# A transformer layer on one core: SyncE's waits for loads and transposes move from ahead of the last eight stores to behind the last transpose

## The chip, the core and the metric

The kernel runs on one core of a Trainium2 chip. The metric is the device time of the whole program in microseconds (us); less is better. Engines are called TensorE (PE), VectorE (DVE), ScalarE (ACT), GpSimd (POOL) and SyncE (SP). SyncE does no arithmetic here: it issues DMA transfers and waits on semaphores, in the order of its queue.

## The reference

One layer of a transformer over 2048 tokens of 448 features, in bfloat16: linear attention with 16 heads of 28, whose feature map is a pair of softmaxes, and a gated feed-forward part of width 1792. Both read a layer norm, and both are added to their input.

```
q, k, v = split(layernorm(x) @ wqkv)                      # 16 heads of 28
phi(a)  = concat(softmax(a @ w_phi), softmax(-(a @ w_phi)))
kv, z   = phi(k)^T @ v, sum(phi(k))
o       = (phi(q) @ kv) / (phi(q) . z + 1e-6)
h       = x + o @ wo
n       = layernorm(h)
out     = h + (sigmoid(n @ w_gate) * (n @ w_up)) @ w_down
```

## The kernel before

The 2048 tokens are 16 tiles of 128 rows. Attention goes tile by tile; the feed-forward part goes by chunks of 2, 4, 4, 4 and 2 tiles (0-1, 2-5, 6-9, 10-13, 14-15). For each chunk TensorE makes the gate and up products (the helper at L514), ScalarE takes tanh (L845), VectorE the product (L852); then, for each tile, TensorE multiplies by `w_down` (L871) into a PSUM bank, VectorE adds that to the residual in `x_sb` (L878, task `fin`), and a DMA writes the tile to the output (L880, task `st`). The two tiles of the last chunk are finished and stored in two parts each: 336 columns (`fina`, `sta`, called wide here) and 112 columns (`finb`, `stb`, narrow).

The kernel is written as a graph of named tasks. `PLAN` is a list of task numbers, written out by hand: the one order in which all tasks are emitted, from which each engine gets its own queue. `emit` walks that list. For each task it first puts into the engine's queue the waits for what the task needs, then the task itself. A wait that the same engine has already made for the same or a higher value is left out (`seen`).

Three kinds of DMA task have rings of semaphores: `in` (24 loads, a semaphore each), `tr` (39 transposes by DMA, 12 semaphores) and `out` (18 stores, 8 semaphores). A task whose ring has gone round waits first for the transfer that used its semaphore before. The walk counts in `nring` how many of each kind it has met. At one point it makes SyncE wait for the last transfer on every `in` and `tr` semaphore: 24 + 12 waits. At the end of the program SyncE waits for the last store on each `out` semaphore.

All loads and transposes and 17 of the 18 stores are in SyncE's queue. By `PLAN` its last part is this, in order (`hT` is the transpose of a normed tile, L810):

```
hT 14, st 5, hT 15, st 8, st 6, sta 15, st 7,
        st 9, st 10, st 12, st 11, st 13, sta 14, stb 14
```

`hT 15` is the last of the 39 transposes. `st 9` is the eleventh store of 18. `stb 15` is in ScalarE's queue, between `sta 14` and `stb 14` in `PLAN`. VectorE's last tasks are, in order, `fin 10`, `fin 12`, `fina 15`, `fin 11`, `fin 13`, `fina 14`, `finb 15`, `finb 14`.

Of the kernel before, what the change touches and what calls it, by code (L numbers as in the profile page):

```python
# [79 lines left out]
class _Graph:  # L80
# [67 lines left out]
    def emit(self, rings):  # L148

        nc = self.nc  # L150
        done = self.planned()
        queues = {e: [] for e in self.ENGINES}
        with ExitStack() as es:
            sems = {e: es.enter_context(nc.semaphore("s_" + e)) for e in self.ENGINES if e != "sp"}
            ring_sems = {k: [es.enter_context(nc.semaphore("s_%s%d" % (k, i))) for i in range(n)]
                         for k, n in rings.items()}
            count = {e: 0 for e in self.ENGINES}
            nring = {k: 0 for k in rings}
            ticket = {}
            seen = {}  # L160

            def wait(eng, sem, key, val):
                if seen.get((eng, key), 0) >= val:
                    return
                seen[(eng, key)] = val
                queues[eng].append(lambda e, sem=sem, val=val: e.wait_ge(sem, val))

            n_out = sum(t.kind == "out" for t in done)
            for t in done:
                if t.kind == "out" and nring.get("out", 0) == n_out - 8:  # L170

                    assert nring["in"] == rings["in"]
                    for k in ("in", "tr"):
                        for j in range(min(nring[k], rings[k])):
                            wait("sp", ring_sems[k][j], (k, j), 16 * ((nring[k] - 1 - j) // rings[k] + 1))
                top = {}
                for d in t.need:
                    sem, key, val, eng = ticket[d]
                    if eng == t.eng == "pe" and d not in t.ordered:
                        continue  # L180
                    if key not in top or top[key][1] < val:
                        top[key] = (sem, val)
                for key, (sem, val) in top.items():
                    wait(t.eng, sem, key, val)
                if t.kind is not None:
                    j = nring[t.kind]
                    nring[t.kind] += 1
                    n = rings[t.kind]
                    sem, key = ring_sems[t.kind][j % n], (t.kind, j % n)
                    if j >= n:  # L190
                        wait(t.eng, sem, key, 16 * (j // n))
                    queues[t.eng].append(lambda e, t=t, sem=sem: t.fn(e).then_inc(sem, 16))
                    ticket[t.name] = (sem, key, 16 * (j // n + 1), "dma")
                else:
                    count[t.eng] += 1
                    sem = sems[t.eng]
                    queues[t.eng].append(lambda e, t=t, sem=sem: t.fn(e).then_inc(sem, 1))
                    ticket[t.name] = (sem, t.eng, count[t.eng], t.eng)

            last = {}  # L200
            for t in done:
                if t.kind == "out":
                    sem, key, val, _ = ticket[t.name]
                    last.pop(key, None)
                    last[key] = (sem, val)
            for key, (sem, val) in last.items():
                wait("sp", sem, key, val)
            with nc.Block() as block:
                starters = {"sp": block.sync, "act": block.scalar, "pe": block.tensor, "dve": block.vector,
                            "pool": block.gpsimd}  # L210
                for e in self.ENGINES:
                    def run(eng, q=queues[e]):
                        for f in q:
                            f(eng)
                    starters[e](run)
# [705 lines left out]
```

## Time and profile before

| | |
|---|---|
| median of 3 runs | 206.84 us (206.36 to 206.85) |
| the profiled execution | 206.24 us |
| its span, first to last instruction | 204.5 us |
| TensorE busy | 196.8 us, 96% of the span |
| VectorE, ScalarE, GpSimd busy | 132.7, 96.0, 79.0 us |
| granted TensorE clock | 1.00 |
| stores on SyncE, issue to landing, median | 1.8 us |

The lines of the profile name an engine, a line of the kernel, an operation and what it writes and reads (`out<-in`). `SPq` is an instruction in SyncE's queue. For a DMA the time shown is that of the issue; its landing is told separately. Times in a timeline count from the first instruction. `EVENT_SEMAPHORE` is an instruction that only waits on semaphores (L166 is the line of the kernel's `wait`); a wait can also be carried by the instruction that it holds. Single records may be missing from a trace.

### The profile page before, as it was taken

The page shows a single profiled execution, that of the slowest core. Times are in us where ns is not written, and L with a number is a line of the kernel's source. Part 1 is how long each engine was busy: PE and PEld are TensorE (multiplying, and loading weights), DVE is VectorE, ACT ScalarE, POOL GpSimd, SP SyncE. Part 2 cuts the span into 40 slices and gives each one's busy share as a digit, 9 for nine tenths or more (in the row PEclk, how much of TensorE's full clock was granted, in tenths as well). Part 3 has the DMA queues.
Part 4 walks back from the last instruction along what each step waited for, and adds up shares of the span by engine and source line. Part 5 has one row for each costly group of instructions (what it writes and reads, how often), then busy time and mean ns, then how long its engine had stood idle before and what let it go on. Part 6 is the DMA issues. An engine that isn't in the chain of part 4 may idle for free.

```text
span 204.5 us, 5003 instructions
## 1 busy us (share of the span) xinstructions
PE 196.8 (96%) x2029; PEld 106.5 (52%) x2029; DVE 132.7 (65%) x306; ACT 96.0 (47%) x182; POOL 79.0 (39%) x141
## 2 busy tenths in 40 slices
PE   7899999999999998999999999999999999999993
PEld 3444454445377764555555544444544444886562
DVE  2999999898799979729574466465128345543033
ACT  3789999998983580423342042423002443551000
POOL 8569999768759865600830003003000300000000
PEclk9999999999999999999999999999999999999999
DMA  5999997059683955191155151013200004000014
GB/s 147 272 268 222 307 383 215 0 110 340 135 132 75 188 88 104 44 168 40 40 114 103 30 103 27 24 27 27 72 0 0 3 11 109 3 3 0 0 42 140
DMA packets 49751, 21.06 MB, mean 103 GB/s; under 512 B 40512, under 2 KB 48704, under 8 KB 49728
## 3 DMA queue, kind: packets, MB, share of 16 engines
q1 hardware_dynamic: 49584, 20.71, 44.6%
q8 instruction: 16, 0.26, 0.5%
q14 instruction: 7, 0.06, 0.1%
q10 hardware_dynamic: 144, 0.03, 0.1%
HBM read 9.20 MB, written 1.84 MB: 54 GB/s over the span
## 4 chain that ended last, share of the span: by engine, by line
PE 76%; ACT 7%; DVE 6%; POOL 5%; issue 2%; DMA 2%; SPq 1%; DVEq 0%; POOLq 0%; ACTq 0%
PE ps L514 51%; PE ps L871 21%; POOL hh L619 3%; ACT eq L654 2%; ACT hh L599 2%; DVE ssum L612 2%; DMA wphK<-in_A_w_phi_dram 2%; PE ps L705 1%; DVE hh L619 1%; POOL rs L543 1%; DVE x_sb L878 1%; PE ps L585 1%; SPq L358 1%; DVE sq L671 1%; PE ps L475 1%
## 5 line engine op out<-in xcount | busy, mean ns | idle before, releaser
L514 PE MATMUL ps<-xT,wg_sb 64*128 64x512 bf16 (+1 forms) x490 | 87.0, 333 | 1.1 <-DVE x_sb L878 0.7
L514 PE MATMUL ps<-xT,wu_sb 64*128 64x512 bf16 (+1 forms) x490 | 86.8, 333 | 0.0
L845 ACT ACTIVATE tg<-ps 128x512 f32<-128x512 f32 (+1 forms) x70 | 33.9, 511 | 76.8 <-PE ps L514 76.1
L852 DVE SCALAR_TENSOR_TENSOR hh<-tg,ps 128x512 bf16<-128x512 f32 (+1 forms) x70 | 38.2, 573 | 32.1 <-ACT tg L845 31.9
L514 PEld LDWEIGHTS ps<-xT,wg_sb 64*128 64x128 bf16 x490 | 45.6, 94 | 22.7 <-issue 1.9
L514 PEld LDWEIGHTS ps<-xT,wu_sb 64*128 64x128 bf16 x490 | 45.6, 94 | 15.2
L871 PE MATMUL ps<-wd_sb,hh 128*128 128x448 bf16 (+2 forms) x252 | 43.5, 332 | 0.0
L871 PEld LDWEIGHTS ps<-wd_sb,hh 128*128 128x128 bf16 x252 | 22.9, 98 | 19.3 <-issue 1.0
L878 DVE SCALAR_TENSOR_TENSOR x_sb<-ps,x_sb 128x448 bf16<-128x448 f32 (+2 forms) x18 | 10.0, 566 | 24.4 <-PE ps L871 24.4
L775 POOL TENSOR_SCALAR rs<-mv 128x1 f32<-128x1 f32 x14 | 2.7, 192 | 59.7 <-DVE mv L774 58.8
L619 POOL TENSOR_TENSOR hh<-hh,rsum 128x896 bf16<-128x896 bf16 x13 | 21.9, 1700 | 0.5 <-DVE rsum L615 0.5
L599 ACT ACTIVATE hh<-ps,rs 128x448 bf16<-128x448 f32 x32 | 18.7, 643 | 2.0 <-PE ps L585 1.1
L654 ACT ACTIVATE eq<-ps,rs 128x448 bf16<-128x448 f32 x32 | 18.1, 649 | 0.0
L612 DVE TENSOR_REDUCE ssum<-hh 128x32 f32<-128x896 bf16 x16 | 16.9, 1058 | 0.8 <-ACT hh L599 0.6
L668 POOL TENSOR_TENSOR halves<-eq 128x448 f32<-128x448 bf16 x14 | 13.4, 970 | 8.3 <-DVE sq L671 2.7
L514 PE MATMUL ps<-Wvc,xT 64*128 64x448 bf16 x112 | 13.2, 351 | 0.2
L681 POOL TENSOR_TENSOR eq<-eq,rq 128x448 bf16<-128x448 bf16 x14 | 13.0, 942 | 1.0 <-DVE eq L681 0.8
L514 PE MATMUL ps<-Wq,xT 64*128 64x448 bf16 x112 | 13.1, 351 | 0.1
L514 PE MATMUL ps<-Wk,xT 64*128 64x448 bf16 x98 | 11.5, 351 | 0.2
L514 PE MATMUL ps<-wo_sb,oT 64*128 64x448 bf16 x98 | 11.3, 350 | 0.1
L790 ACT ACTIVATE hn<-x_sb,nb,rs 128x512 bf16<-128x512 bf16 x10 | 7.8, 810 | 5.5 <-POOL nb L788 3.0
L715 DVE TENSOR_TENSOR o_pad<-ps,rden 128x448 bf16<-128x448 f32 x16 | 9.8, 620 | 0.2
(104 smaller groups left out, 186.4 us busy)
## 6 DMA issues: line engine op xcount, KB each, us to landing
wu_sb<-in_B_w_up_dram SPq DMA_DIRECT2D x2, 896.0 KB, 8.2
wg_sb<-in_B_w_gate_dram SPq DMA_DIRECT2D x2, 896.0 KB, 7.5
out_dram<-x_sb SPq DMA_DIRECT2D x14, 112.0 KB, 1.8
x_sb<-in_A_x_dram SPq DMA_DIRECT2D x3, 448.0 KB, 4.1
wd_sb<-in_B_w_down_dram SPq DMA_DIRECT2D x3, 448.0 KB, 4.6
hh<-in_A_wqkv_dram SPq DMA_DIRECT2D x4, 196.0 KB, 3.6
wo_sb<-in_A_wo_dram SPq DMA_DIRECT2D x2, 336.0 KB, 9.5
x_sb<-in_A_x_dram SPq DMA_DIRECT2D x2, 224.0 KB, 4.0
```

The lines of the kernel that those rows point to most:

```text
L514: r = e.matmul(ap(), lhsT=st(blk, rows), rhs=mv(blk, rows), start=first and i == 0, stop=not first and i == 2, tile_position=(rows.start, 0))
L599: task((key, t), "act", 0.53, lambda e, t=t, s=s, i=i, b=kb: e.activation(signs(ek[:, s, :])[:, :, :, i, :], heads2(bank[b()][:, 0:D]), AC ...
L612: task(("ss", t), "dve", 1.0, lambda e, s=s: e.tensor_reduce(ssum[:, s, :], ek[:, s, :].rearrange("p (h d) -> p h d", d=DH), AX.X, ALU.add ...
L619: return e.tensor_tensor(phi[:, t % NPHI, :, 0:GP].rearrange("p k (a d) -> p k a d", d=DH), ek[:, s, :].rearrange("p (k a d) -> p k a d", ...
L654: task((key, t), "act", 0.53, lambda e, w=w, t=t, i=i, b=bk[j]: e.activation(signs4(eq[:, w, :, 0:GP])[:, :, :, i, :], heads2(bank[b()][:, ...
L668: task(("hs", t), "pool", 0.9, lambda e, w=w, half_=half_, by4=by4: e.tensor_tensor(half_, by4(eq[:, w, :, 0:GP])[:, :, :, 0:DH // 2], by4 ...
L681: return e.tensor_tensor(ap, ap, rq[:, w, :].rearrange("p (k h) -> p k h", h=2)[:, :, :, None].to_broadcast([P, NPAIR, 2, DH]), ALU.mult)
L715: task(("o", t), "dve", 0.56, lambda e, t=t, res=res: e.tensor_tensor(o_pad[:, t % 4, 64 * (t % 2):64 * (t % 2) + D].rearrange("p (h d) -> ...
L845: task(("tg", c, f_), "act", 0.51 if n == 4 else 0.3, lambda e, j=j, N=N, b=gb[i]: e.activation(tg[:, j % NSG, 0:N], bank[b()][:, 0:N], AC ...
L852: e.scalar_tensor_tensor(hhT[c % 2][:, f_, 0:N], tg[:, j % NSG, 0:N], 1.0, bank[b()][:, 0:N], op0=ALU.add, op1=ALU.mult), deps)
L871: r = e.matmul(bank[b][:, cols], lhsT=hhT[c % 2][:, f_, ts], rhs=wd_sb[:, f_, cols], start=(f_ == 0), stop=(f_ == FT - 1))
L878: e.scalar_tensor_tensor(X(t)[:, cols], bank[got(first)[0]][:, cols], 0.5, X(t)[:, cols], op0=ALU.mult, op1=ALU.add), [nm, ("hn", t)])
```

## The change

`emit` put the block of waits ahead of the store that leaves eight stores to come, itself included, that is ahead of the eleventh (`n_out - 8` is 10). The changed walk puts it ahead of the first store that it meets when all 24 loads and all 39 transposes have been met, and then not again. The waits themselves, their number and their order are as before, and so is `PLAN`.

```diff
-            n_out = sum(t.kind == "out" for t in done)
+            n_tr, checked = sum(t.kind == "tr" for t in done), False
             for t in done:
-                if t.kind == "out" and nring.get("out", 0) == n_out - 8:
-
-                    assert nring["in"] == rings["in"]
+                if t.kind == "out" and nring["in"] == rings["in"] and nring["tr"] == n_tr and not checked:
+
+                    checked = True
                     for k in ("in", "tr"):
                         for j in range(min(nring[k], rings[k])):
                             wait("sp", ring_sems[k][j], (k, j), 16 * ((nring[k] - 1 - j) // rings[k] + 1))
```

## The prediction

> **What bounds the kernel now.** I read the page first, then the chain of waits over the last 20 us, then SyncE's own queue store by store, and last VectorE's timeline beside it. The page says that TensorE is busy nearly throughout, and the end of the chain says what it hands over to:
>
> ```profile
> span 204.5 us, 5003 instructions
> PE 196.8 (96%) x2029; PEld 106.5 (52%) x2029; DVE 132.7 (65%) x306; ACT 96.0 (47%) x182; POOL 79.0 (39%) x141
> 185.33 15.39 PE ps L871 x98
> 200.75 0.69 DVE x_sb L878 x2
> 201.44 0.27 DVE x_sb L878
> ```
>
> The last computing instruction ends at 201.44 + 0.27 = 201.71 us, but the span ends at 204.5. The chain starts at the last compute instruction, so it does not show the 2.8 us behind it. Those belong to the stores and to the waits for their landing. The change edits SyncE's queue, so the question is whether that stretch is set by the last result (201.71 plus one store) or by the queue. SyncE's timeline, cut into short windows so that every store has its own line, answers it (start, duration of the issue):
>
> ```profile
> 197.64 0.33 SPq L880 DMA_DIRECT2D out_dram<-x_sb  x1
> 198.01 0.43 SPq L880 DMA_DIRECT2D out_dram<-x_sb  x1
> 199.62 0.33 SPq L880 DMA_DIRECT2D out_dram<-x_sb  x1
> 200.00 0.42 SPq L880 DMA_DIRECT2D out_dram<-x_sb  x1
> 200.47 0.45 SPq L880 DMA_DIRECT2D out_dram<-x_sb  x1
> 201.03 0.39 SPq L880 DMA_DIRECT2D out_dram<-x_sb  x1
> 201.53 0.39 SPq L880 DMA_DIRECT2D out_dram<-x_sb  x1
> 202.01 0.41 SPq L880 DMA_DIRECT2D out_dram<-x_sb  x1
> 202.51 0.40 SPq L880 DMA_DIRECT2D out_dram<-x_sb  x1
> ```
>
> By the order written in the kernel these nine are: the wide half of tile 15, tile 7, then tiles 9, 10, 12, 11, 13, then the wide and the narrow half of tile 14. (The narrow half of tile 15 goes out on ScalarE.) They follow each other with no free time except between 198.44 and 199.62, ahead of tile 9, the eleventh store in the order: just where the old kernel puts its block of waits. VectorE's timeline gives when each result is there (tiles 7 and 9 are not among them: they were finished long before):
>
> ```profile
> 188.12 0.62 DVE L878 SCALAR_TENSOR_TENSOR x_sb<-ps,x_sb 128x448 bf16<-128x448 f32 x1 [1.91 <-PE ps L871]
> 194.42 0.62 DVE L878 SCALAR_TENSOR_TENSOR x_sb<-ps,x_sb 128x448 bf16<-128x448 f32 x1 [5.01 <-PE ps L871]
> 197.10 0.51 DVE L878 SCALAR_TENSOR_TENSOR x_sb<-ps,x_sb 128x336 bf16<-128x336 f32 x1 [2.06 <-PE ps L871]
> 197.53 0.61 DVE L878 SCALAR_TENSOR_TENSOR x_sb<-ps,x_sb 128x448 bf16<-128x448 f32 x1
> 199.75 0.62 DVE L878 SCALAR_TENSOR_TENSOR x_sb<-ps,x_sb 128x448 bf16<-128x448 f32 x1 [1.61 <-PE ps L871]
> 200.75 0.51 DVE L878 SCALAR_TENSOR_TENSOR x_sb<-ps,x_sb 128x336 bf16<-128x336 f32 x1 [0.37 <-PE ps L871]
> 201.17 0.26 DVE L878 SCALAR_TENSOR_TENSOR x_sb<-ps,x_sb 128x112 bf16<-128x112 f32 x1
> 201.44 0.27 DVE L878 SCALAR_TENSOR_TENSOR x_sb<-ps,x_sb 128x112 bf16<-128x112 f32 x1
> ```
>
> In order: tiles 10, 12, 15 wide, 11, 13, 14 wide, 15 narrow, 14 narrow. The last store was issued at 202.51 although its data were ready at 201.71: for 0.80 us it waited for nothing but its turn. Once SyncE is released at 197.62 by tile 15, it is the queue that bounds the end, not TensorE or VectorE. This is what decides the case: work taken out of that queue shortens the kernel, up to the 0.80 us.
>
> **What the change removes.** The block of waits is one wait for each of 24 load semaphores and 12 transpose semaphores. In the trace it is this row, asked for between 198.46 and 199.60 (duration min/median/max, first and last start):
>
> ```profile
> L166 SPq EVENT_SEMAPHORE  x18: 27/28/28, 198.5 to 199.5; - x18
> ```
>
> Eighteen records hold 36 waits, so two go in one record. All are for transfers that landed long ago, so none waits; each costs only its passage. Eighteen in the 1.18 us from 198.44 to 199.62, less the gap of about 0.05 that stands between any two stores (200.42 to 200.47), make 1.13 us, or 0.063 us each, of which 0.028 is in the record itself. This 1.13 us leaves the end of the queue.
>
> **Where it goes.** The new condition first holds at the first store behind the last of the 39 transposes. That is tile 8, directly behind the transpose of tile 15:
>
> ```profile
> 169.19 1.20 SPq L810 DMA_TRANSPOSE xT<-hn  x1
> 170.44 1.04 SPq L880 DMA_DIRECT2D out_dram<-x_sb  x2
> DMA to landing us min/median/max: 2.4/2.4/2.4
> SPq L880 <- DVE x_sb L878: 26.1, 1, 26.1
> ```
>
> The third row is the landing of that one transpose: 169.19 + 2.4 = 171.6. Now the block does one thing more than before, because its last wait is for a transfer still in flight. SyncE would pass the other waits by 170.44 + 1.13 = 171.57, so it is held to about 171.65 and issues tile 8 some 1.2 us later than now; tile 6 follows it. Queued behind them on SyncE are only the end's stores, and the fourth row says that SyncE then stands 26.1 us, from 171.5 to 197.62, for tile 15's result. The 1.2 us disappear in that; 25 us of cover are left. No compute waits for stores 8 and 6 (x_sb is not written again for these tiles); only the stores of tiles 13 and 14 wide, which reuse their semaphores, do, 28 us later. The moved waits therefore cost nothing. The Trainium skill (DMA: Bandwidth & Descriptors, "Rules for kernel authors") says to issue a transfer early and wait on its semaphore late. That speaks against the new place, and by that rule alone the price would be the 1.2 us above; the 26.1 us row says that here "late" is the crowded place and "early" the empty one.
>
> **The end rebuilt.** Pitches from the rows: store to store 0.47 (200.00 to 200.47), with one wait record between 0.56, 0.50, 0.48 and 0.50; tile 12 to 11 and all later ones keep theirs, which are waits for older stores. From tile 7 at 198.01: tile 9 at 198.48, tile 10 at 198.95, tile 12 at 199.42, tile 11 at 199.98, tile 13 at 200.48 (its result: 199.75 + 0.62 = 200.37, just in time). Tile 14 wide could go at 200.96, but its result comes at 200.75 + 0.51 = 201.26: now VectorE is late, and SyncE waits 0.3 us. It goes at 201.28, and tile 14 narrow 0.44 to 0.50 later (the short issue of 0.33 after a wait, as at 197.64, or the usual one), at 201.72 to 201.78. That is not ahead of its own result at 201.71. Against 202.51 the last issue is 0.73 to 0.79 us earlier; I take 0.75. So of 1.13 us removed, about a third is eaten by the wait for tile 14's wide half, and the next thing that is late is TensorE's last group through VectorE.
>
> What follows the last issue:
>
> ```profile
> DMA to landing us min/median/max: 1.5/1.5/1.5
> L880 ACTq DMA_DIRECT2D out_dram<-x_sb x1: 400/400/400, 201.5 to 201.5; - x1
> out_dram<-x_sb ACTq DMA_DIRECT2D x1, 28.0 KB, 1.6
> L166 SPq EVENT_SEMAPHORE  x4: 17/28/28, 203.4 to 204.0; - x4
> L208 PEldq EVENT_SEMAPHORE  x1: 51/51/51, 204.5 to 204.5; - x1
> ```
>
> The first row is the last store's: 202.51 + 1.5 = 204.0, where the last of the four closing waits passes, and 0.5 us later the program is over. Changed: 201.76 + 1.5 = 203.26, end at 203.75. ScalarE's store, issued at 201.5, lands 1.6 later, at 203.1, and does not bind. The span becomes 203.75. The profiled execution took 206.24 us beside its span of 204.5; 1.74 lies around it and is untouched, so it would take 205.5. The three timed runs have 206.36 to 206.85, median 206.84: minus 0.75 that is 206.1, or 0.36% less.
>
> **Rivals.**
>
> *The waits are dear only in the trace.* Of 0.063 us for a record 0.028 is execution; if the rest came from recording, the block would cost 18 x 0.028 = 0.5 us in an untraced run, and the last issue would be at 202.51 - 0.63 = 201.88 before and at 201.76 after. The gain would be about 0.1 us: no change. Against it: the traced execution, 206.24, is not slower than the untraced ones.
>
> *The denser burst lands later.* With the pause gone, seven stores follow each other without a break and share the 16 DMA engines with each other and with ScalarE's store. If that delays the last landing beyond 204.0, the kernel gets slower. The point is a time to landing of 204.0 - 201.76 = 2.24 us for the last store, and 2.9 us for a loss of over 0.3%. For it:
>
> ```profile
> DMA to landing us min/median/max: 1.5/1.8/2.4
> 197.60:202.95 5.35, 3.80 (x33) 2.35 (x30) 2.12 (x6) 0.00 (x0) 0.00 (x0) 1.00 0.46 150
> DMA to landing us min/median/max: 1.5/1.7/1.9
> ```
>
> The first row is over all stores: the slowest took 2.4 us, and with this for the last one the end would come 0.14 us later than now. Against it: the second row has the DMA engines busy for 0.46 of the burst; taking 1.13 us out makes it 0.46 x 5.35 / 4.22 = 0.58. And in the third, the ten stores from 197.64 on, seven of them already at the closest pitch, never took over 1.9. The Trainium skill (DMA: Bandwidth & Descriptors, "Latency and other measured facts") gives HBM's access latency as 0.2 us on average and 2 us at high load, and calls it the main part of a transfer's fixed cost. By that rule, an estimate of 1.8 us more for the last landing would make the end 203.75 + 1.8 = 205.55, one microsecond later than now; the spread of 1.5 to 1.9 in the burst does not bear it out.
>
> *The change leaves the end as it is.* If the block stood elsewhere than I read, say still behind tile 15's store, the time would stay at 206.8. Against it: all 24 loads and 39 transposes stand ahead of tile 8 in the order, so the condition can't hold later. Some other shift of the same size belongs here as well: the untouched kernel's own runs differ by 0.49 us.
>
> **How the numbers follow.** About 0.3%, 0.62 us, is what a measurement of this kernel can tell from no change, and my 0.75 is only just beyond it. Forecast (the queue shortens, VectorE takes over): 0.70, of which 0.60 shows as faster and 0.10 falls short of 0.62. Waits cheap outside the trace: 0.14, within 0.3%. Denser burst: 0.08, of which 0.05 slower by over 0.3%. No effect or another shift: 0.08, of which 0.02 slower. Together faster 0.60, same 0.33, slower 0.07. The range runs from the fastest run less the most that the queue can give, 206.36 - 0.80 = 205.6, to no gain at the slowest run, 206.85; I put 205.5 and 206.9.
>
> **What would show it.** In the profile of the changed kernel, SyncE should have the 18 wait records at about 170.4 to 171.6 and the store of tile 8 at 171.7; from 197.6 on, nine stores with no pause over 0.1 us except one of some 0.3 us before tile 14's wide half, released by VectorE; the last issue near 201.75, the last landing near 203.25, the span near 203.75; TensorE and VectorE as before up to 201.7. The forecast is wrong if the block is still in the burst, if the last issue is early but its landing is not, or if tile 15's result comes at another time.

## The result and the profile after

The changed kernel takes 205.95 us (median, 205.62 to 206.21) against 206.73 us for the old one in the same comparison (206.36 to 206.95): a ratio of 0.9958, 95% interval 0.9946 to 0.9969. That is 0.78 us or 0.42% less. On record were 206.1 us and 0.75 us less.

The profiled execution took 205.88 us, with these lines on its page and at the end of its chain of waits (start, duration, what):

```profile
span 204.1 us, 5001 instructions
185.73 15.39 PE ps L871 x98
201.14 0.69 DVE x_sb L878 x2
201.83 0.28 DVE x_sb L878
```

The span is only 0.4 us shorter, not 0.75. The reason is ahead of the change: VectorE's last result stands at 201.83 + 0.28 = 202.11 us, 0.4 us later than in the old kernel's profile, and TensorE's closing group of 15.39 us starts 0.4 us later too. So does the last transpose, which stands in SyncE's queue ahead of the block's new place: it is issued at 169.59 us, in the old kernel at 169.19. What the change can touch lies behind that result. There the old kernel needed 204.5 - 201.71 = 2.8 us and the new one needs 204.1 - 202.11 = 2.0 us. This "end behind the last result" is the number to follow below, since it is free of what happened earlier in an execution.

First the new place of the block. The lines are the wait records between 170.82 and 172.64 (duration, first and last start), the wait among them from the list of SyncE's waits (us in total, times, longest), and the store behind them from its timeline:

```profile
L166 SPq EVENT_SEMAPHORE  x18: 17/28/28, 170.8 to 172.6; - x18
SPq L166 <- DMA xT<-hn: 0.7, 1, 0.7
172.66 0.33 SPq L880 DMA_DIRECT2D out_dram<-x_sb  x1
```

The eighteen records are there, SyncE stands 0.7 us for the last transpose, and tile 8 goes out at 172.66. Then SyncE waits for the burst, and this is the burst:

```profile
SPq L880 <- DVE x_sb L878: 25.4, 3, 24.5
198.03 0.33 SPq L880 DMA_DIRECT2D out_dram<-x_sb  x1
198.41 0.43 SPq L880 DMA_DIRECT2D out_dram<-x_sb  x1
198.88 0.43 SPq L880 DMA_DIRECT2D out_dram<-x_sb  x1
199.36 0.46 SPq L880 DMA_DIRECT2D out_dram<-x_sb  x1
199.86 0.45 SPq L880 DMA_DIRECT2D out_dram<-x_sb  x1
200.41 0.39 SPq L880 DMA_DIRECT2D out_dram<-x_sb  x1
200.90 0.40 SPq L880 DMA_DIRECT2D out_dram<-x_sb  x1
201.68 0.33 SPq L880 DMA_DIRECT2D out_dram<-x_sb  x1
202.13 0.35 SPq L880 DMA_DIRECT2D out_dram<-x_sb  x1
```

The hole of 1.18 us between the second and the third store is gone (198.41 + 0.43 to 198.88). The only hole left, from 201.30 to 201.68, is before tile 14's wide half, whose result comes at 201.14 + 0.51 = 201.65. The last store is issued at 202.13, 0.02 behind its own result at 202.11; in the old kernel it was 0.80 behind.

### The profile page after: what moved, and what is told of

Its sections match the earlier page's. It is cut to its first block, busy times and chain, and to the rows that moved or that the text cites. A ratio compares the mean times of both kernels' runs of the same rounds, so it can differ in the third digit from the quotient of the medians.

```text
span 204.1 us, 5001 instructions
## 1 busy us (share of the span) xinstructions
PE 196.5 (96%) x2027; PEld 106.1 (52%) x2029; DVE 132.8 (65%) x306; ACT 96.0 (47%) x182; POOL 78.8 (39%) x141
## 4 chain that ended last, share of the span: by engine, by line
PE 74%; ACT 7%; DVE 6%; POOL 5%; SPq 3%; DMA 2%; issue 2%; DVEq 0%; POOLq 0%; ACTq 0%
PE ps L514 51%; PE ps L871 21%; POOL hh L619 3%; ACT eq L654 2%; ACT hh L599 2%; DMA xT<-in_A_x_dram 2%; SPq L358 2%; DVE ssum L612 2%; PE ps L705 1%; DVE hh L619 1%; POOL rs L543 1%; DVE x_sb L878 1%; SPq L363 1%; DVE sq L671 1%; DVE o_pad L715 1%
```

## Experiments

Two accounts were put against each other. The **queue theory** is the prediction's: wait records cost about 0.06 us each where SyncE's queue is the bound, that is in the burst of the last nine stores, and nothing elsewhere. The **early-check theory** says that the gain comes from what the block does at its new place: it holds two stores back and settles the last transpose early. Beside them stood other readings of the old place, as the expectations name them.

**No block.**

```diff
-                if t.kind == "out" and nring.get("out", 0) == n_out - 8:
-                    ...
```

> The block of 36 waits is left out altogether; nothing else is changed. Queue theory (only wait records that stand in SyncE's queue ahead of the last stores, in the burst from 197.6 us on, cost time): as the changed kernel, about 205.95 us, and the program ends 2.0 us behind VectorE's last result (old kernel 2.8). Early-check theory (the gain comes from what the block does at its new place: it holds the stores of tiles 8 and 6 back by some 2 us and makes sure of the last transpose): no gain without it, about 206.7 us, end 2.8 us behind the last result.

205.80 us against 206.56 us, ratio 0.996 (0.9947 to 0.9974). The page, the last piece of the chain of waits and the last store:

```profile
span 204.6 us, 4983 instructions
201.58 0.96 DVE x_sb L872 x3
202.57 0.35 SPq L874 DMA_DIRECT2D out_dram<-x_sb  x1
```

The last store is 0.03 us behind its result, and the end is 204.6 - 202.54 = 2.1 us behind it. The whole gain is there with nothing at the new place, so the early-check theory falls.

**Block ahead of the ninth store.**

```diff
-                if t.kind == "out" and nring.get("out", 0) == n_out - 8:
+                if t.kind == "out" and nring.get("out", 0) == 8:
```

> The block stands ahead of the ninth store (tile 15 wide), behind the stores of tiles 8 and 6, which then go out as early as in the old kernel. SyncE has 26 us of idle time at that place. Queue theory: as the changed kernel, 205.95 us, end 2.0 us behind the last result. Early-check theory: as the old kernel, 206.7 us and 2.8 us, since stores 8 and 6 are not held back.

205.82 us, ratio 0.9957 (0.9944 to 0.997); end 204.0 - 201.97 = 2.0 us behind the last result. Two stores earlier in the queue than the old place, ahead of the store for which SyncE waits long, is worth as much as the change. The block's last two records pass only behind that wait, at 197.90 and 197.96. That makes the burst start 0.1 us later, and the pause before tile 14's wide half is as much shorter.

**Block behind all stores.**

```diff
-                if t.kind == "out" and nring.get("out", 0) == n_out - 8:
-                    ...
+            for k in ("in", "tr"):
+                for j in range(min(nring[k], rings[k])):
+                    wait("sp", ring_sems[k][j], (k, j), 16 * ((nring[k] - 1 - j) // rings[k] + 1))
             last = {}
```

> The block stands behind all stores, ahead of the closing waits. Queue theory: the 18 records take 1.1 us while the last store is in flight for 1.5 us, so nearly all of it is hidden: end 2.0 to 2.2 us behind the last result, 205.95 to 206.1 us. If instead the records cost their 1.1 us wherever they stand late in the queue: 2.8 to 3.1 us behind the last result, about 206.8 us.

205.93 us, ratio 0.9965 (0.995 to 0.998). The page, the last piece of the chain of waits, the last store, and the wait records from 202.9 on, the closing waits among them:

```profile
span 204.7 us, 5001 instructions
201.60 0.96 DVE x_sb L875 x3
202.59 0.35 SPq L877 DMA_DIRECT2D out_dram<-x_sb  x1
L166 SPq EVENT_SEMAPHORE  x22: 17/28/28, 203.0 to 204.3; - x22
```

The records run from 203.0 to 204.3, nearly all of them while the last store is under way (202.59 plus some 1.5 us); the last two pass behind its landing. The end is 204.7 - 202.56 = 2.1 us behind the last result, from the unrounded times 2.17, about 0.1 more than in the changed kernel: work for SyncE is hidden behind a landing as well as in a wait, as far as the landing lasts.

**Block deeper in the burst.**

```diff
-                if t.kind == "out" and nring.get("out", 0) == n_out - 8:
+                if t.kind == "out" and nring.get("out", 0) == 15:
```

> The block stands deeper in the burst, ahead of the sixteenth store (tile 14 wide). Queue theory: the last two stores are late by as much as in the old kernel, end 2.7 to 2.8 us behind the last result, about 206.7 us: within the burst the place does not matter. If the old place was bad because it held back seven stores, and made them crowd later, the loss would be less here, with only two stores behind it: end 2.2 to 2.5 us behind the last result, 206.1 to 206.4 us.

206.55 us, ratio 1.0 (0.9987 to 1.0014): the old time. The same lines:

```profile
span 205.1 us, 5001 instructions
201.30 0.96 DVE x_sb L878 x3
L166 SPq EVENT_SEMAPHORE  x20: 17/28/28, 201.5 to 203.0; - x20
203.10 0.38 SPq L880 DMA_DIRECT2D out_dram<-x_sb  x1
```

Nineteen of the twenty records stand ahead of tile 14's wide half and one behind it. Last result at 202.26, last store at 203.10, 0.84 behind it, end 2.8 us behind. With two stores behind the block instead of seven the loss is the same, so what counts is that the records stand in the queue while it runs without a gap, not how many stores they hold back.

**Six of eighteen records stay.** Ahead of the eleventh store only the waits of one ring are made, the other ring's ahead of the seventh.

```diff
+                if t.kind == "out" and nring.get("out", 0) in (6, n_out - 8):
+                    k = {6: "in", n_out - 8: "tr"}[nring["out"]]
```

> Dose: the 12 transpose waits (6 records) stay ahead of the eleventh store, the 24 load waits go ahead of the seventh. Queue theory with the cap at tile 14 wide: 6 x 0.061 = 0.37 us, less about 0.1 for the shorter issue behind a wait, just fill the 0.3 us that SyncE waits for tile 14 wide in the changed kernel: end 2.0 to 2.1 us behind the last result, 205.95 to 206.05 us. If the cost is simply proportional with no cap: a third of 0.78 lost, end 2.3 us behind, 206.2 us.

205.68 us against 206.46 us, ratio 0.9955 (0.9942 to 0.9968): nothing lost against the changed kernel. The same three lines:

```profile
span 204.3 us, 5001 instructions
201.18 0.96 DVE x_sb L876 x3
202.19 0.40 SPq L878 DMA_DIRECT2D out_dram<-x_sb  x1
```

The last store is 0.05 us behind its result, and the end 204.3 - 202.14 = 2.2 us (2.13 from the unrounded times, just over the range expected; the account without a cap wanted 2.3). The cap is there, a limit on what taking records out can bring: the hole before tile 14's wide half takes up six records.

**Twelve of eighteen stay.**

```diff
-                    k = {6: "in", n_out - 8: "tr"}[nring["out"]]
+                    k = {6: "tr", n_out - 8: "in"}[nring["out"]]
```

> Dose: the 24 load waits (12 records) stay ahead of the eleventh store, the 12 transpose waits go ahead of the seventh. Queue theory with the cap: 0.73 - 0.1 - 0.3 = 0.3 to 0.4 us more than the changed kernel, end 2.3 to 2.4 us behind the last result, 206.3 us. Proportional without a cap: two thirds of 0.78, end 2.55 us behind, 206.5 us.

206.11 us, ratio 0.9983 (0.9971 to 0.9995).

```profile
span 204.4 us, 5001 instructions
201.03 0.96 DVE x_sb L876 x3
202.41 0.40 SPq L878 DMA_DIRECT2D out_dram<-x_sb  x1
```

The last store is 202.41 - 201.99 = 0.42 us behind its result, the end 2.4. Twelve records cost 0.42 us, eighteen 0.80: six more for 0.38, at 0.06 each.

**Block twice.**

```diff
+                    for k in ("in", "tr"):
+                        for j in range(min(nring[k], rings[k])):
+                            sem, val = ring_sems[k][j], 16 * ((nring[k] - 1 - j) // rings[k] + 1)
+                            queues["sp"].append(lambda e, sem=sem, val=val: e.wait_ge(sem, val))
```

> Dose: the old kernel with the block put in twice at the old place (36 records). Queue theory: the whole second block counts, 18 x 0.061 = 1.1 us: end 3.8 to 3.9 us behind the last result, 207.8 us. If the waits in the burst were cheap and the old kernel was late for another reason: 2.8 to 2.9 us, 206.8 us.

207.43 us, ratio 1.0048 (1.003 to 1.0065), slower by 0.97 us.

```profile
span 205.4 us, 5019 instructions
200.51 0.96 DVE x_sb L882 x3
203.36 0.39 SPq L884 DMA_DIRECT2D out_dram<-x_sb  x1
```

The last store is 203.36 - 201.47 = 1.89 us behind its result, 1.09 more than in the old kernel, for 18 more records: 0.061 us each, with no cap any more. The end is 3.9 us behind. The medians grew by 0.97 us where 1.1 was expected.

**Stores reordered, block not moved.** In the written order the store of tile 15 wide goes behind that of tile 12.

```diff
-... 895 889 1034 892 898 957 963 960 966 ...
+... 895 889 892 898 957 963 1034 960 966 ...
```

> The old kernel with the block still ahead of its eleventh store, but in the written order the store of tile 15 wide stands behind that of tile 12, so that the stores of tiles 7, 9, 10 and 12 no longer queue behind it. The eleventh store is then tile 9 or 10, at a time when SyncE is idle. Queue theory: the block is passed long before the burst, end 2.0 us behind the last result, 205.95 us, without moving the block. If the eleventh place itself or the number of waits set the loss: as the old kernel, 2.8 us and 206.7 us.

205.79 us, ratio 0.9969 (0.9954 to 0.9984).

```profile
span 203.9 us, 5003 instructions
L176 SPq EVENT_SEMAPHORE  x19: 17/28/28, 172.6 to 188.9; - x19
200.83 0.96 DVE x_sb L888 x3
201.82 0.35 SPq L890 DMA_DIRECT2D out_dram<-x_sb  x1
```

The block is still ahead of the eleventh store, but that store (tile 10) now waits for a result at 188.8: all but two of the records are past before that wait, and the last two by 189. The end is 203.9 - 201.79 = 2.1 us behind the last result. The eleventh place was bad only because the written order had filled the queue there.

## Why the prediction was right

*The queue bounds the end.* Shown: records taken out of the burst, by five different edits with the change among them, bring the last store from 0.80 us to 0.02 to 0.03 us behind its result; records put in push it out by 0.061 us each.

*The price of a record.* 0.063 us was read from the hole; 0.061 came out of the doubled block. In the executions as recorded, a record holds the queue for more than twice the 0.028 us that it lasts itself.

*The cap.* The prediction let tile 14's wide half eat a third of the 1.13 us and gave 0.73 to 0.79 us. Measured: the last issue went from 0.80 to 0.02 us behind its result, 0.78. The doses of six and twelve show the cap by itself. The pause before tile 14's wide half was 0.38 us, not some 0.3. Put 0.39 us later, by as much as tile 15's store came later, the rebuilt end gives the place of each of the nine stores to within 0.05 us.

*The number.* That 0.75 on record and 0.78 in the medians lie so close is in part luck: the interval of the ratio allows 0.64 to 1.12 us. The firmer witness is the end behind the last result, 2.80 us before and 2.04 after from the unrounded times: 0.76 us.

*A sign of being wrong that came up.* The forecast was to be wrong if tile 15's result came at another time. Its store went out at 198.03 instead of 197.64, and so the last issue, the last landing and the span all came 0.4 us later than the marks on record. But the last transpose, ahead of everything that the change moves, was late by 0.40 us too, so this shift is not the change's doing; the last section has what lies behind it.

*The moved block costs nothing.* True, but one size was off. Tile 8 was to go out some 1.2 us later than before, as soon as the transpose had landed. It went out 172.66 - (169.59 + 1.19) = 1.88 us behind the issue of the last transpose, where it was 0.05 before. The wait for that transpose is not the block's last but its ninth record, so half the records come after it. SyncE's wait for tile 15 was still 24.5 us, and the run without any block is no faster. The Trainium skill (DMA: Bandwidth & Descriptors, "Rules for kernel authors") has the rule to wait late on a transfer's semaphore. Waiting early cost nothing measurable at this place.

*The denser burst.* Its landings, all ten from 198 us on and the last two, and the DMA engines' share in it (the last number but one of the third line):

```profile
DMA to landing us min/median/max: 1.5/1.8/1.8
DMA to landing us min/median/max: 1.5/1.6/1.6
198.00:202.55 4.55, 3.79 (x33) 2.35 (x30) 2.12 (x6) 0.00 (x0) 0.00 (x0) 1.00 0.51 171
```

No store took longer than the 1.9 us of before, at a share of 0.51 instead of 0.46 (0.58 was expected). The rival falls. The latency at high load in the same page of the Trainium skill ("Latency and other measured facts") is not reached here.

*Waits that are dear only in the trace.* Not settled: each timed run comes with a span of its own, so all of them may have been recorded. The argument on record against this rival, that the traced execution is no slower than untraced ones, falls with that, and what the records cost with nothing recorded isn't known. What is known is that the medians moved by 0.78 us, as much as the end behind the last result did in the traces.

What now follows the last result is one issue, one landing of 1.5 us and the closing. Taking waits out of SyncE's queue has no more to give: none of the versions that empty it as far or further ends less than 2.0 us behind the last result, and none is clearly faster than the changed kernel.

## What to carry to other kernels

The chain of waits ends at the last computing instruction; look at what stands between that and the end of the span, and list the store queue one store at a time. A wait that is long satisfied is not free: in SyncE's queue here, where it ran without a gap, each record was a delay of 0.06 us for all that followed, and it cost nothing where the queue waited anyhow, ahead of a long wait or, but for some 0.1 us, behind the last issue. Before a gain is counted, ask which result is late next; here that result kept back a third of what was removed.

## What the runs showed beyond that

Much of the difference between two spans does not come from the end. In the ten kernels, whose instructions are the same up to the last transpose, VectorE's last result came at 201.47 to 202.56 us, and in all ten it stands 32.46 to 32.52 us behind the issue of the last transpose: what parts them is earlier. Three of them at VectorE's third and fourth statistics of `x`, the old kernel, the changed one and the one with the block behind all stores:

```profile
9.36 1.14 DVE L533 BATCH_NORM_STATS2 st<-x_sb 128x6 f32<-128x448 bf16 x2
9.87 1.15 DVE L533 BATCH_NORM_STATS2 st<-x_sb 128x6 f32<-128x448 bf16 x2 [0.59 <-DMA x_sb<-in_A_x_dram]
10.22 1.15 DVE L530 BATCH_NORM_STATS2 st<-x_sb 128x6 f32<-128x448 bf16 x2 [0.83 <-DMA x_sb<-in_A_x_dram]
```

Their last results stand at 201.71, 202.11 and 202.56. The load of `x` behind them is issued at 4.80 us in all three and lands at 9.23, 9.84 and 10.20. That it lands some tenths later shows again at the end of the kernel: 0.51 and 0.86 us here, 0.40 and 0.85 there. In the other seven the two shifts differ by up to 0.3 us, so this load is not the only source, and no run holds it fixed. For a change worth 0.8 us at the end, one span says little. The time from the last result to the end tells it to a few hundredths: from the unrounded times it is 2.04 to 2.06 us in the four kernels that have the block ahead of SyncE's long waits or not at all, and 2.80 in the old one.
